# Strassen's algorithm for the first channel product of batches 4 to 7 and of the tail chunk of a fused attention and mixer kernel

## The chip, the cores and the metric

The kernel runs on one core of one Trainium2 chip. The metric is the device time of one execution in microseconds; the median of three runs of the kernel before is 276.59 us (276.38 to 277.32). A kernel is a fixed program for each engine: PE (TensorE) multiplies matrices, DVE (VectorE), ACT (ScalarE) and POOL (GpSimd) work elementwise, SP (SyncE) issues transfers. Each engine runs its own list in order, and waits on semaphores for the others.

## The reference, cut to what matters

Random-feature attention over 8 batches of 8 heads, 576 rows of 64, and then a mixer that multiplies over the rows (token product) and over the 512 channels (channel products, 512 to 1536 and back).

```python
# phi(x) = exp(x @ omega.T - |x|^2/2 - max) / sqrt(128), of q and k scaled
kv = np.einsum('bhsm,bhsd->bhmd', k_p, v)
z = np.sum(k_p, axis=2)
num = np.einsum('bhsm,bhmd->bhsd', q_p, kv)
den = np.einsum('bhsm,bhm->bhs', q_p, z)[..., None] + 1e-06
...
x = np.ascontiguousarray(attn_out.transpose(0, 2, 1, 3)).reshape(B, S, H * D)
xt = x.transpose(0, 2, 1)
h = np.maximum(xt @ w_tok1, 0.0) @ w_tok2
u = x + h.transpose(0, 2, 1)
h2 = np.maximum(u @ w_ch1, 0.0) @ w_ch2
return (u + h2).astype(np.float32)
```

## The kernel before

**Stages.** Each batch passes through attention (`attention`), the token product (`token_mix`, lines 763 to 800) and the channel products (`channel_mix`, line 955). The first 512 rows of each batch form a chunk of 512; the last 64 rows of all eight batches together form a ninth one, the tail chunk, with c equal to 8 in the code. All large operands are float16; TensorE sums in float32 in PSUM, which is handed out as eight banks of 128 x 512.

**The first channel product** (line 966) takes twelve output blocks of 128 channels. Each is four matmuls of 512 columns into one bank (weights `wc1`, moving data `t_uT`, the transposed rows), after which ACT or DVE applies the relu and writes float16 into `t_r3`.

**The second channel product** of batches 1 to 7 and of the tail (`channel_out_fast`, line 857) already goes by Strassen's algorithm: seven products of half-size matrices in place of eight, with sums of weights prepared once (`t_T`, line 448) and sums of `t_r3` made for each chunk into the single buffer `t_S` and into `t_r3` itself (line 878, through the helper on line 295). Each product is twelve matmuls of 256 columns (line 916). Three banks X, Y and Z collect the products, DVE reads them out (line 905) into `t_o`, and a transfer stores them.

**Order.** Nothing is scheduled by the framework. Every piece of work is a `Job`, added with an engine, a cost, the jobs that it depends on, and the ring places that it takes and gives back. The list `ORDER` gives the order of all jobs by their numbers (a negative one is a warming matmul), `SLOT` the places taken, and `MOVED` the jobs that run on another engine than the usual one. These three tables are the result of a planner that ran beforehand; the text of the kernel holds only its answer. Each engine gets its instructions in the sequence of `ORDER`, so a long instruction or a wait on one engine holds up everything later on it.

**Rings.** `COUNT` gives the number of buffers: 3 for the transposed q and k of a batch (`qT`, `kT`), 4 for the exponentials `qp` and `kp`, 3 for the token relu `r1`, 3 for `uT`, 2 for `r3`. The reciprocals of the attention sit in buffers that are chosen by parity (`t_km[hp % 2]`, `t_rc[2 + hp % 2]`).

**Transfers.** Chunk c's rows `t_u` (line 793, four DVE additions) are transposed by a transfer on SP's queue into `t_uT` (line 798). The same queue brings in `kT` and `qT` of later batches. POOL issues the loads of v and the casts of q and k, and between them multiplies v by its weights (`vs`, `vbd`, line 295).

Of the kernel before, what the change touches and what calls it, by code (L numbers as in the profile page):

```python
# [81 lines left out]
]  # L82
SLOT = (
    "0100234050607011034025217063304156020014123024233037016112506321174115613214067030406102530471612141"
    "6710324016307250311067345122353640751421105324100325261073641220501046112501420700521173142350120702"
    "6123534100753141200127003221065413207102503410160022357312126034171542176210025011041121126022037516"
# [82 lines left out]
def kernel(  # L169
# [27 lines left out]
    R = SM // 2  # L197
    RT = ST // 2
    RA = R + RT
    NPE = 2  # L200
    RW = S * 4 // P
    c_scale = float(1.0 / math.sqrt(math.sqrt(D)))

# [93 lines left out]
    def bank(name):  # L297
        return banks[place("bank", name)]
# [772 lines left out]
```

## Time and profile before

| | |
|---|---|
| median of 3 runs | 276.59 us |
| the profiled execution, first to last instruction | 275.9 us |
| PE busy | 266.6 us, 2503 matmuls |
| DVE busy | 222.9 us, 462 instructions |
| ACT busy | 138.1 us, 289 instructions |
| POOL busy | 91.2 us, 115 instructions |
| moved by DMA | 39.66 MB |

The profiled execution's own device time isn't given apart from its span; the runs' median lies 0.7 us above the span. Busy time is the union of an engine's instructions. On DVE the end of one instruction overlaps the start of the next by some 0.08 us, so that in a dense row the step from one start to the next is shorter than the duration. The same holds far more for PE: the duration of a matmul includes its passage through the array, and its rate is read from the length of a long row of equal ones.

### The profile page before, as it was taken

Reading aid. Unit: us, or ns where it says so; the run is one execution under the profiler, and the core shown is the slowest. Engines: PE = TensorE matmul, PEld = TensorE weight load, DVE = VectorE, ACT = ScalarE, POOL = GpSimd, SP = SyncE. Lnnn points to the kernel's source line nnn. Section 1 sums busy time; section 2 is a strip of 40 time slices with the busy share of each in tenths; the row PEclk is TensorE's granted clock in tenths of the full one; section 3 lists DMA queues with packets and bytes.
Section 4 is the critical chain, followed back from the end, with each engine's and each line's share of the span. In section 5 each row is a group of like instructions: output and inputs, shape, how many; then the busy total and the mean of one; then the engine's idle time right before and its main releaser. Section 6 shows DMA issues by size and latency. Waiting matters only on the chain.

```text
span 275.9 us, 6228 instructions
## 1 busy us (share of the span) xinstructions
PE 266.6 (97%) x2503; PEld 165.5 (60%) x2503; DVE 222.9 (81%) x462; ACT 138.1 (50%) x289; POOL 91.2 (33%) x115
## 2 busy tenths in 40 slices
PE   8789999999999999999999999999999999999993
PEld 3367455444567655755676656755676477446782
DVE  3897889876998799987999899978985992675992
ACT  3999941188685338734756456636654500040200
POOL 8994492063703490075019510600043000000001
PEclk9999999999999999999999999999999999999998
DMA  7999999999998999979989994840252304021125
GB/s 195 192 209 212 190 212 177 202 193 146 203 191 133 229 176 186 151 148 171 198 184 183 232 125 123 191 90 2 97 79 77 96 0 95 2 99 53 78 83 146
DMA packets 81292, 39.66 MB, mean 144 GB/s; under 512 B 63984, under 2 KB 77040, under 8 KB 81072
## 3 DMA queue, kind: packets, MB, share of 16 engines
q0 software_dynamic: 31744, 17.74, 44.2%
q1 hardware_dynamic: 47072, 15.50, 28.7%
q10 hardware_dynamic: 2448, 6.03, 5.6%
q8 instruction: 19, 0.31, 0.5%
q14 instruction: 9, 0.07, 0.1%
HBM read 35.95 MB, written 16.52 MB: 190 GB/s over the span
## 4 chain that ended last, share of the span: by engine, by line
PE 89%; DMA 6%; POOL 3%; DVE 0%; issue 0%; POOLq 0%
PE bank L966 33%; PE bank L916 25%; PE bank L777 5%; PE bank L790 5%; DMA w1m<-in_moe_w_tok_dram 4%; PE bank L1000 4%; PE bank L734 3%; PE bank L656 3%; PE bank L668 2%; PE bank L701 2%; DMA uT<-u 2%; POOL r L319 1%; PE bank L844 1%; PE bank L816 1%; PE bank L828 1%; PE bank L736 1%
## 5 line engine op out<-in xcount | busy, mean ns | idle before, releaser
L966 PE MATMUL bank<-uT,wc 128*128 128x512 f16 x376 | 90.4, 379 | 0.3 <-DMA uT<-u 0.3
L290 ACT ACTIVATE r<-bank 128x512 f16<-128x512 f32 (+1 forms) x84 | 46.9, 597 | 77.1 <-PE bank L966 62.0
L295 POOL TENSOR_TENSOR vs<-v,vs 128x512 f16<-128x512 f16 x31 | 33.2, 1074 | 91.2 <-DVE vs L682 60.5
L966 PEld LDWEIGHTS <-wc 128*128 128x128 f16 x424 | 38.3, 98 | 37.9 <-issue 1.1
L916 PEld LDWEIGHTS <-r 128*128 128x128 f16 x384 | 36.9, 98 | 8.1 <-issue 1.2
L514 ACT ACTIVATE kp<-bank 128x512 f16<-128x512 f32 x64 | 35.6, 622 | 10.4 <-PE bank L656 10.4
L514 ACT ACTIVATE qp<-bank 128x512 f16<-128x512 f32 x64 | 36.3, 616 | 8.9 <-PE bank L668 6.0
L680 DVE TENSOR_REDUCE km<-kp 128x8 f16<-128x1024 f16 x32 | 38.6, 1206 | 2.5 <-ACT kp L514 2.4
L292 DVE TENSOR_SCALAR r<-bank 128x512 f16<-128x512 f32 (+1 forms) x42 | 27.7, 672 | 12.0 <-PE bank L966 11.2
L744 DVE TENSOR_TENSOR x<-bank,rc 128x320 f16<-128x320 f32 x62 | 30.5, 492 | 2.1
L916 PEld LDWEIGHTS <-S 128*128 128x128 f16 x288 | 27.9, 98 | 5.4 <-issue 0.3
L905 DVE TENSOR_TENSOR o<-u,bank 128x512 f32<-128x512 f16 x28 | 19.0, 679 | 6.9 <-PE bank L916 6.8
L916 PE MATMUL bank<-T,r 128*128 128x256 f16 x192 | 23.8, 273 | 0.0
L916 PE MATMUL bank<-T,S 128*128 128x256 f16 x192 | 23.6, 273 | 0.0
L916 PE MATMUL bank<-wc,r 128*128 128x256 f16 x192 | 23.6, 273 | 0.0
L945 POOL DMA_DIRECT2D out_dram<-o x2 | 1.3, 648 | 60.9 <-issue 60.9
L793 DVE TENSOR_TENSOR u<-x,bank 128x512 f16<-128x512 f16 x28 | 17.8, 681 | 1.1 <-PE bank L790 1.0
L905 DVE TENSOR_TENSOR o<-o,bank 128x512 f32<-128x512 f32 (+1 forms) x27 | 16.6, 618 | 2.2 <-PE bank L916 1.6
L734 PEld LDWEIGHTS <-qp 128*128 128x128 f16 x256 | 13.8, 98 | 7.0 <-DVE kvsb L286 0.2
L734 PE MATMUL bank<-kvsb,qp 128*128 128x65 f16 x256 | 15.6, 193 | 0.0
L743 DVE RECIPROCAL rc<-bank 128x5 f32<-128x5 f32 x62 | 11.5, 186 | 4.1 <-PE bank L736 2.7
L701 PEld LDWEIGHTS <-kp 128*128 128x128 f16 x256 | 11.5, 98 | 5.1
(120 smaller groups left out, 376.3 us busy)
## 6 DMA issues: line engine op xcount, KB each, us to landing
out_dram<-o ACTq DMA_DIRECT2D x9, 512.0 KB, 2.6
q<-in_q_dram POOLq DMA_DIRECT2D x6, 576.0 KB, 7.2
wc<-in_moe_w_ch_dram POOLq DMA_DIRECT2D x4, 768.0 KB, 10.6
k<-in_k_dram POOLq DMA_DIRECT2D x6, 512.0 KB, 6.9
v<-in_v_dram POOLq DMA_DIRECT2D x6, 512.0 KB, 8.9
out_dram<-o SPq DMA_DIRECT2D x5, 512.0 KB, 3.9
r<-in_q_dram POOLq DMA_DIRECT2D x4, 288.0 KB, 7.3
v<-in_v_dram POOLq DMA_DIRECT2D x4, 256.0 KB, 8.7
```

The source lines that it names most:

```text
L290: nc.scalar.activation(out=out, in_=in_, func=AF.Relu)
L292: nc.vector.tensor_relu(out=out, in_=in_)
L295: (nc.gpsimd if eng == "POOL" else nc.vector).tensor_tensor(**kw)
L514: nc.scalar.activation(out=out, in_=in_, func=AF.Exp, bias=0.0, scale=1.0)
L680: nc.vector.reduce_max(out=mx, in_=kpv, axis=AX.X)
L701: nc.tensor.matmul(ps[:, i, :], kpv[:, 2 * i + j // 2, j % 2, :], vs[:, i * NJ + j, 0 : D + 1], start=(i == 0 and j == 0), stop=False, ski ...
L734: nc.tensor.matmul(ps[:, k, j * 65 : (j + 1) * 65], st, s[:, i, 0 : D + 1], start=True, stop=True)
L744: nc.vector.tensor_tensor(out=t_x[place("x", b)][:, :, (2 * hp + hs[0]) * D : (2 * hp + hs[0] + n) * D].rearrange("p j (i d) -> p i j d", ...
L793: nc.vector.tensor_tensor(out=t_u[place("u", b)][:, j, :], in0=t_x[place("x", b)][:, j, :], in1=bank(n), op=ALU.add)
L905: nc.vector.tensor_tensor(out=o, in0=a, in1=ps, op=ALU.add)
L916: nc.tensor.matmul(ps[:, j * DH : (j + 1) * DH], a[:, cb, j * P : (j + 1) * P], w[:, cb, :], start=(bank_of(b, j0) not in held and j == j0 ...
L966: nc.tensor.matmul(ps, wc1[:, db, cb * P : (cb + 1) * P], moving(db), start=(db == 0), stop=(db == ND - 1))
```

## The change

**The first channel product of chunks 4 to 8** no longer runs as 48 matmuls of 512 columns. A new function `channel_in_fast` splits rows, inner and outer dimension in halves and forms seven products P1 to P7 in place of eight, in three groups of 256 output channels. Each product of a group is four matmuls of 256 columns. Bank X takes P1, then P6 on top of it, P7 on top of both, and P4 at last; ACT copies what stands in X after each of the first three to SBUF in float32, because the next product changes it. Y takes P2, Z takes P5 and P3. DVE adds each copy to the bank that belongs to it (`join`) and the relu follows: of one quarter straight from the bank, of the other three on float16 in SBUF. The copies of P1 go into the part of `r3` that the same group fills later, the others into places of the `qp` and `kp` rings.

**Sums.** Four sums of blocks of `uT` are made for each chunk, in a place of the `uT` ring, and four sums of weights (in two parts each) once for all, in `weight_sums`: three parts in a place of `qT`, three in one of `kT`, held until the end, and two in a new buffer.

**The rest.** `r1` has 2 places in place of 3. Reciprocals `km`, `kmt` and `rc` become ring buffers with 4, 2 and 8 places, taken and given back by jobs, and the reciprocal and the scaling become jobs of their own; the scaling may go to ACT. The tail's output uses places of `x` in place of `o`. The sums of the second product have looser dependences among them. `ORDER`, `SLOT` and `MOVED` are new throughout; with them 13 of the 64 sums of the second product move from DVE to POOL, 5 of the 8 sums of weights and 11 of the 20 sums of `uT` are put there, and 35 more scalings of 128 x 64 run on ACT. The branches for `SPLIT` and `HALVES` aren't taken, since both are empty.

```diff
+    FAST_IN = 4
+    SPLIT = ()
+    HALVES = ()
...
-             "kvsb": 3, "ktt": 2, "x": 3, "r1": 3, "u": 3, "uT": 3, "r3": 2, "S": 1, "o": 2, "bank": 8}
+             "kvsb": 3, "ktt": 2, "x": 3, "r1": 2, "u": 3, "uT": 3, "r3": 2, "S": 1, "o": 2, "km": 4, "rc": 8, "kmt": 2, "bank": 8}
...
+    def weight_sums(key):
...
+        steps = (((1, 0), (1, 1), ALU.add), (0, (0, 0), ALU.subtract), ((0, 0), (1, 0), ALU.subtract), ((0, 1), 1, ALU.subtract))
+        for a in range(2):
+            done = []
+            for i, (x, y, op) in enumerate(steps):
+                e_sum = engine("DVE")
...
+    def channel_in_fast(c, key, jt):
...
+        ops = {
+            "P1": ("X", weights(0, 0), lambda: block(0, 0), []),
+            "P2": ("Y", weights(0, 1), lambda: block(1, 0), []),
+            "P5": ("Z", sum_weights(0), lambda: sums()[:, 0], [j_sums[0][0], j_sums[1][0], j_s[0]]),
+            "P6": ("X", sum_weights(1), lambda: sums()[:, 1], [j_sums[0][1], j_sums[1][1], j_s[1]]),
+            "P7": ("X", sum_weights(2), lambda: sums()[:, 2], [j_sums[0][2], j_sums[1][2], j_s[2]]),
+            "P4": ("X", weights(1, 1), lambda: sums()[:, 3], [j_s[3]]),
+            "P3": ("Z", sum_weights(3), lambda: block(1, 1), [j_sums[0][3], j_sums[1][3]]),
+        }
...
+                            nc.tensor.matmul(ps[:, n, :], w(a)[:, (2 * m + n) * P : (2 * m + n + 1) * P], x_[:, a],
+                                             start=(what in ("P1", "P2", "P5") and n == 0 and a == 0), stop=False, skip_group_check=True)
...
+            p1 = product("P1", [])
+            p2 = product("P2", [])
+            p5 = product("P5", [])
+            k1 = keep("P1", "X", p1)
+            c11 = join("P1", "Y", 0, 0, [k1, p2], True)
+            p6 = product("P6", [k1])
+            k2 = keep("U2", "X", p6)
+            p7 = product("P7", [k2])
+            k3 = keep("U3", "X", p7)
+            c22 = join("U3", "Z", 1, 1, [k3, p5, c11], False)
+            p3 = product("P3", [c22])
+            c12 = join("U2", "Z", 0, 1, [k2, p3], True)
+            p4 = product("P4", [k3])
...
     def channel_mix(c, key, jt):
...
+        if c >= FAST_IN:
+            channel_out_fast(c, key, channel_in_fast(c, key, jt))
+            return
...
+        if b == FAST_IN:
+            weight_sums(b - 1.0)
```

More of the change, by code (lines that the diff above doesn't have):

```diff
@@ L598, in kt_max @@
                 )
-            j_ktm = add("DVE", 1.2, kkt + 0.01, kt_max, deps=[*j_kte, j_msk], take=[("vbd", b)] if dma_in else [])
+            j_ktm = add("DVE", 0.15, kkt + 0.01, kt_mask, deps=[j_ktm, j_msk], take=take_vbd, give=[("kmt", b)])
             def vbd():
@@ new lines, in rec, with scale @@
+                def rec(hp=hp, i=hs[0], where=where):
+                    nc.vector.reciprocal(out=t_rc[place("rc", (b, hp, i))], in_=where()[:, 0, 0 : 5 * 65].rearrange("p (j d) -> p j d", d=65)[:, :, D])
+                j_r = add("DVE", 0.1, kno, rec, deps=[j_n], take=[("rc", (b, hp, hs[0]))])
+                e_num = engine("DVE")
+                def scale(hp=hp, i=hs[0], where=where, e_num=e_num):
+                    to = t_x[place("x", b)][:, :, (2 * hp + i) * D : (2 * hp + i + 1) * D]
+                    ps = where()[:, 0, 0 : 5 * 65].rearrange("p (j d) -> p j d", d=65)[:, :, 0:D]
+                    rc = t_rc[place("rc", (b, hp, i))]
+                    if e_num == "ACT":
+                        for j in range(NJ + 1):
+                            nc.scalar.activation(out=to[:, j], in_=ps[:, j], func=AF.Copy, scale=rc[:, j : j + 1])
+                    else:
+                        nc.vector.tensor_tensor(out=to, in0=ps, in1=rc.unsqueeze(2).broadcast_to((P, NJ + 1, D)), op=ALU.mult)
@@ L762, in attention @@
+                last_x.append(add(e_num, 0.45, kno, scale, deps=[j_r], take=[("x", b)], give=[at, ("rc", (b, hp, hs[0]))]))
         return last_x
@@ L865, in channel_out_fast @@
             part = slice(g * NH // 2, (g + 1) * NH // 2)
-            need = [jr[cb + NH * e] for cb in range(part.start, part.stop) for e in range(2)]
+            need = [x for cb in range(part.start, part.stop) for e in range(2) for x in jr[cb + NH * e]]
             steps = (
@@ L878, in go @@
                     tt(e_sum, out=o[:, part], in0=a[:, part], in1=b[:, part], op=op)
[L879 to L880 removed]
+                job = add(e_sum, 0.5, key + KEYS["S"] + 0.1 * g + 0.01 * k, go, deps=[*need, *([done[2 if k == 3 else 0]] if k else [])], take=[("S", c)])
+                done.append(job)
                 sums.setdefault(i, []).append(job)
@@ L897, in bank_of, with o_tag, o_of, go @@
             return (b, c, j0) if tail else (b, c)
+        def o_tag(i):
+            return ("x", ("o", i)) if tail else ("o", (c, i))
+        def o_of(i):
+            if tail:
+                return t_x[place(*o_tag(i))].rearrange("p j d -> p (j d)")[:, 0 : 4 * DM].bitcast(FP32).rearrange("p (j d) -> p j d", j=2)
+            return t_o[place(*o_tag(i))]
         def read(k, b, i, e, base, deps, free, j0=0, j1=2):
-            def go(c=c):
-                o = t_o[place("o", (c, i))][:, j0:j1, DH * e : DH * e + DH]
+            e_read = engine("DVE")
+            def go(c=c, e_read=e_read):
+                o = o_of(i)[:, j0:j1, DH * e : DH * e + DH]
                 ps = bank(bank_of(b, j0)).rearrange("p (j d) -> p j d", j=2)[:, j0:j1]
+                if e_read == "ACT":
+                    nc.scalar.copy(out=o, in_=ps)
+                    return
                 u = t_u[place("u", c)] if c < B else t_ut
@@ L905, in go, with late_base, base_in @@
                 nc.vector.tensor_tensor(out=o, in0=a, in1=ps, op=ALU.add)
-            return add("DVE", 0.345 * (j1 - j0), key + KEYS["c2"] + step * k, go, deps=deps, take=[("o", (c, i))],
+            return add(e_read, 0.345 * (j1 - j0), key + KEYS["c2"] + step * k, go, deps=deps, take=[o_tag(i)],
                        give=([("bank", bank_of(b, j0))] if free else []) + ([("u", c)] if base and c < B else []))
+        def late_base(k, i, e, x, deps):
+            e_base = engine("POOL")
+            def base_in(c=c, x=x, e_base=e_base):
+                if outs[x, 0].eng == "DVE":
+                    return
+                o = o_of(i)[:, :, DH * e : DH * e + DH]
+                tt(e_base, out=o, in0=t_u[place("u", c)][:, 2 * i : 2 * i + 2, DH * e : DH * e + DH], in1=o, op=ALU.add)
+            return add(e_base, 1.1, key + KEYS["c2"] + step * k, base_in, deps=deps, give=[("u", c)])
         outs, j_z = {}, {}
@@ L944, in store @@
                         to = out[4 * i : 4 * i + 4, SM:S, cols].rearrange("(j h) t d -> h t j d", h=2)[h]
-                        (nc.scalar if eng == "ACT" else nc.sync if eng == "SP" else nc.gpsimd).dma_start(out=to[:, js], in_=t_o[place("o", (c, i))][half[h], js, cols])
-                    dma(eng, key + 0.9, 0.3, store, deps=[outs[need, j] for j in range(*js)], give=[("o", (c, i))],
+                        (nc.scalar if eng == "ACT" else nc.sync if eng == "SP" else nc.gpsimd).dma_start(out=to[:, js], in_=o_of(i)[half[h], js, cols])
+                    dma(eng, key + 0.9, 0.3, store, deps=[outs[need, j] for j in range(*js)], give=[o_tag(i)],
                         cost=0.412 if js[1] - js[0] == 1 else 0.414)
@@ L951, in store @@
             def store(i=i, eng=eng):
-                (nc.scalar if eng == "ACT" else nc.sync).dma_start(out=out[c, 0:SM, :].rearrange("(p j) d -> p j d", j=NJ)[:, 2 * i : 2 * i + 2, :], in_=t_o[place("o", (c, i))])
-            dma(eng, key + 0.9 + 0.1 * i, 1.3, store, deps=[outs[x, 0] for x in need], give=[("o", (c, i))], cost=0.4)
+                (nc.scalar if eng == "ACT" else nc.sync).dma_start(out=out[c, 0:SM, :].rearrange("(p j) d -> p j d", j=NJ)[:, 2 * i : 2 * i + 2, :], in_=o_of(i))
@@ L984, in relu @@
                 relu_to(e_relu, t_r3[place("r3", c)][:, cb, :], bank(n))
-            jr[cb] = (add(e_relu, 0.5, key + 0.5 * pos / NCB, relu, deps=[j1], take=[("r3", c)], give=[("bank", n)]))
+            jr[cb] = [add(e_relu, 0.5, key + 0.5 * pos / NCB, relu, deps=[j1], take=[("r3", c)], give=[("bank", n)])]
         if fast:
@@ L1001, in channel_mix @@
                 prev = add("PE", mm(4, 512) + (mm(4, P) if part == 2 else 0.0), key + 0.5 + 0.5 * (3 * j + part) / 12, c2,
-                           deps=[prev, *jr[4 * part : 4 * part + 4], *j_wc2], take=[("bank", n)], give=[("r3", c), ("uT", c)])
+                           deps=[prev, *(x for done in jr[4 * part : 4 * part + 4] for x in done), *j_wc2], take=[("bank", n)], give=[("r3", c), ("uT", c)])
             k2 = key + 0.5 + 0.5 * (3 * j + 3) / 12
```

208 lines of the change are left out of this document (150 added, 58 removed), and 131 rows, old and new, of the table ORDER.

## The prediction

> **What bounds the kernel now.** I read the page first, then the chain of work that ended last in order of time.
>
> ```profile
> span 275.9 us, 6228 instructions
> PE 266.6 (97%) x2503; PEld 165.5 (60%) x2503; DVE 222.9 (81%) x462; ACT 138.1 (50%) x289; POOL 91.2 (33%) x115
> PE 89%; DMA 6%; POOL 3%; DVE 0%; issue 0%; POOLq 0%
> ```
> ```profile
> 83.37 5.98 DMA uT<-u
> ...
> 234.09 13.81 PE bank L966 x64
> ...
> 260.94 10.51 PE bank L916 x96
> 271.48 0.42 DVE o L905
> ```
>
> The chain is TensorE almost throughout. Two of its long rows give the rates: a matmul of 512 columns takes 13.81 / 64 = 0.2158 us, one of 256 columns 10.51 / 96 = 0.1095 us. The other engines appear with the head's loads, with one transposing transfer (5.98 us from the last addition of `u` to the first matmul on it) and with the last read. The stretches from the end of one batch's token product to the next's show how near the others come:
>
> ```profile
> 109.86:139.12 29.26, 29.26 (x294) 18.73 (x293) 25.80 (x54) 17.44 (x38) 9.58 (x11) 1.00 0.95 172
> 139.12:167.34 28.22, 28.22 (x266) 17.93 (x265) 25.77 (x56) 15.06 (x31) 12.19 (x14) 1.00 1.05 181
> 167.34:196.46 29.12, 29.12 (x274) 18.26 (x273) 25.45 (x52) 16.26 (x34) 4.86 (x5) 1.00 0.44 101
> 196.46:224.50 28.04, 28.04 (x260) 17.73 (x259) 23.44 (x50) 13.16 (x27) 5.20 (x5) 1.00 0.30 67
> 224.50:275.90 51.40, 46.94 (x336) 32.64 (x334) 32.66 (x61) 5.92 (x11) 1.29 (x2) 0.98 0.25 75
> ```
>
> The columns are the stretch, then busy PE, weight loads, DVE, ACT and POOL, and the clock. PE is never idle in four of them, at full clock; DVE is busy for 100.5 of 114.6 us there (88%), ACT for 54% and POOL for 28%. So a saving on TensorE counts in full until DVE becomes the later one. That is the question of this change.
>
> **TensorE.** Five chunks lose 48 matmuls of 512 columns each and gain 84 of 256 (seven products, three groups, four matmuls): 240 x 0.2158 = 51.8 us go and 420 x 0.1095 = 46.0 us come, together **-5.8 us**. The new ones load weights as often as those of L916, whose loads hide:
>
> ```profile
> L916 PEld LDWEIGHTS <-r 128*128 128x128 f16 x384 | 36.9, 98 | 8.1 <-issue 1.2
> ```
>
> 98 ns stand under 109.5 ns of matmul. If that cover went, the 11 ns of difference show how little it would need, but the same pair already runs at the rate above. PE's other work keeps its sizes, and its order is much the same up to the token product of batch 2.
>
> **DVE.** Durations overlap, so I take steps from one start to the next:
>
> ```profile
> 216.02 0.49 DVE L744 TENSOR_TENSOR x<-bank,rc 128x320 f16<-128x320 f32 x1
> 216.42 0.18 DVE L743 RECIPROCAL rc<-bank 128x5 f32<-128x5 f32 x1
> 223.43 1.88 DVE L793 TENSOR_TENSOR u<-x,bank 128x512 f16<-128x512 f16 x3
> ```
> ```profile
> 248.18 0.55 DVE L295 TENSOR_TENSOR S<-S,r 128x768 f16<-128x768 f16 x1
> 248.65 0.55 DVE L295 TENSOR_TENSOR r<-r 128x768 f16<-128x768 f16 x1
> ```
> ```profile
> L292 DVE TENSOR_SCALAR r<-bank 128x512 f16<-128x512 f32 x40 | 26.9, 684 | 11.7 <-PE bank L966 11.2
> L905 DVE TENSOR_TENSOR o<-o,bank 128x512 f32<-128x512 f32 x21 | 14.1, 674 | 1.6 <-PE bank L916 1.1 <-issue 0.2
> L680 DVE TENSOR_REDUCE km<-kp 128x8 f16<-128x1024 f16 x32 | 38.6, 1206 | 2.5 <-ACT kp L514 2.4
> L545 DVE COPY ktt<-kT 128x256 f16<-128x256 f16 x1 | 0.2, 227 | 0.0
> ```
>
> Three additions with a PSUM operand of 512 take 1.88 us and one lasts 0.68, so the step is (1.88 - 0.68) / 2 = 0.60 us; the scaling steps by 0.40, a sum of 768 float16 values in SBUF by 0.47, which is 0.61 ns per value. Away go 20 relus from PSUM (12.0 us), 13 sums of the second product (6.1) and 7 scalings (2.8): 20.9 us. There come 45 joins, float32 with a bank as the L905 row (27.0), one relu from PSUM (0.6), three sums of weights (1.4), nine sums of 512 of `uT` (2.8), and seven relus each of 1024 and 512 values in SBUF. The trace has no such relu. Below, the copy of 256 values in 0.23 us bounds each; above, the reduction of 1024 with 1.21 us and the 0.68 us row for 512. At 0.61 ns per value they are 0.63 and 0.31, together 6.6 us (bounds 3.2 and 13.2). In all DVE gains 38.4 - 20.9 = **17.5 us** (14 to 24). Counted by the order of the two programs, some 4 of it fall between the token products of batches 3 and 7, where TensorE's share shrinks by 6 at the same time, and the rest behind. There DVE goes from 88% busy to 96%, and in the last stretch from 32.7 to about 46 of some 51 us. It still fits, barely, and only if nothing is late.
>
> **ACT and POOL.**
>
> ```profile
> 205.90 3.09 POOL L295 TENSOR_TENSOR vs<-v,vs 128x512 f16<-128x512 f16 x3 [0.42 <-DVE vs L682]
> ```
> ```profile
> 208.08 1.58 ACT L290 ACTIVATE r<-bank 128x512 f16<-128x512 f32 x3
> ```
> ```profile
> L756 ACT ACTIVATE x<-bank,rc 128x64 f16<-128x64 f32 x10 | 2.3, 340 | 0.0
> ```
>
> ACT steps by 0.49 us for 512 values, POOL by 1.02 (three in 1.58 and in 3.09, less one of 0.60 and of 1.06). ACT gains 45 copies and loses 26 relus from banks, 9.3 us; 35 short scalings add 8.0 at 0.23 each, and eight relus each of 1024 and 512 values in SBUF some 10 at its own rate: 27 us onto 68 of the last 166, no bound. POOL gains 18 sums of 768 (1.52 each) and 11 of 512, 38.6 us onto 33.1 of 166: not a bound either, but its sums feed products of TensorE, and it issues the loads of v and the casts behind them in the same list. The cover is POOL's idle time, 82.8 of the 114.6 us of the four stretches; if it failed, whatever stands behind a sum would come 1.52 us later for each.
>
> **Where TensorE now waits.** I followed three places in the new order.
>
> (1) The sums S2 of chunk 6. Between the last P3 of that chunk and the first matmul on the second half of S2, TensorE has 8 matmuls on half rows, 8 of 512 and 47 of 256 columns: 0.4 + 1.7 + 5.1 = 7.2 us. In that time DVE has two joins, six additions from PSUM, two sums S1, a read of the output and three sums: 9 x 0.60 + 5 x 0.47 = 7.8 us. It is 0.6 us late.
>
> (2) The transfer of chunk 7. It begins with the last addition of `u`, which ends 1.5 us behind the last token product since DVE has the joins ahead of it. At 5.98 us it lands 7.5 us behind; TensorE has 60 matmuls of 256 columns, 6.6 us, and the 0.6 of (1). That leaves 0.3 us.
>
> (3) The tail's S2. POOL makes S1 and S2 of one half, 2 x 1.52 = 3.0 us, behind a relu on ACT that comes after three long ones. TensorE reaches the first matmul on it about 0.7 us earlier.
>
> That is 1.6 us. Chunks 4, 5 and the start of 6 have the same pattern with attention between to fill it; I add 0.9, so **+2.5 us**. Bounds are 0 (all hidden, as before the change) and 0.6 in each of 15 groups, 9.0.
>
> **Edits at nothing.** The reciprocals' ring takes a wait off DVE at most: 0 to -0.5 us, covered by TensorE. The second place less of `qT`, `kT` and `r1` makes transposed loads on SP wait for TensorE's use two batches back; the uT transfer stands behind them on the same queue. The cover is that these loads are due a batch ahead; without it the 5.98 us of the transfer would be late once more, and TensorE with it.
>
> **Sum.** Span 275.9 - 5.8 + 2.5 = 272.6 us. The runs' median is 276.59, 0.7 above the profiled span, so 273.3 us is expected for the median.
>
> **Rivals.** *No new waits.* The order hides everything as the old one did: 275.9 - 5.8 + 0.7 = 270.8 us. For it speaks that TensorE is never idle in four stretches with DVE at 88%, against it the three places above. Chance 0.18.
>
> *The chain within a group eats the saving.* Each group goes product, copy, product, copy, product, copy, join, product, join, relu: 4 x 0.44 us of products, 3 x 0.60 of copies and 3 x 0.68, with a change of engine at nine steps, so over 5.6 us, while it holds up to three of eight banks. If other work does not fill it, 15 groups each lose 0.4 us: 6.0 in place of 2.5 gives 276.8 us, no change. Chance 0.13.
>
> *DVE and POOL stop each other (slower).* In the one place of the head where both multiply data in SBUF at once, POOL's product took 0.44 us longer:
>
> ```profile
> 14.52 1.02 DVE L295 TENSOR_TENSOR vs<-v,vs 128x512 f16<-128x512 f16 x1
> ...
> 14.96 1.50 POOL L295 TENSOR_TENSOR vs<-v,vs 128x512 f16<-128x512 f16 x1
> ```
>
> Elsewhere the old kernel hardly puts the two at once: its POOL products run in the attention, its sums behind. The new one gives POOL 29 sums, and DVE has 26 sums and relus of float16 in SBUF between the token products of batches 3 and 7. If each of those waits for half a POOL sum, 0.75 us, DVE gets 19.5 us more; some 11 of them is the room that is left, and 8.5 go to TensorE: 275.9 - 5.8 + 8.5 + 0.7 = 279.3 us. It decides from about nine hits on above the room, 6.6 us of new waits. Against it speaks that many of these sums wait for one another anyway. Chance 0.15.
>
> The Trainium skill (SBUF — State Buffer, Who interferes with whom) states this as a rule: a VectorE instruction with two inputs in SBUF and a GpSimd instruction that reads SBUF exclude each other, and the second to issue waits for the whole of the first. The trace agrees as far as its one case goes: 0.44 us longer with 0.58 us of the DVE product left.
>
> **How the numbers follow.** The forecast has 0.50 (271.8 to 275 us, its waits between 1 and 4), the rivals 0.18, 0.13 and 0.15, and 0.04 is left for others. What a measurement tells from no change is 0.3%, 275.8 to 277.4 us. Faster: 0.50 + 0.18 + 0.02 = 0.70; same 0.13; slower 0.15 + 0.02 = 0.17. The range 270.5 to 277.8 takes in the forecast, both nearer cases and a weak form of the last.
>
> **What would show it.** In the new profile the 84 matmuls per chunk should step by 0.110 us, and PE's sum fall by 5.8. DVE should be over 90% busy from batch 3's token product on, and the joins take 0.67 us each. The chain should show DVE or POOL ahead of the second products of chunks 6 and 8, for under 1 us each, and the transfer of chunk 7. POOL sums of 768 far above 1.5 us, or DVE sums above 0.56, would speak for the third rival; many gaps ahead of P6, P7 and P3 for the second. A TensorE that waits at the start of a chunk for a transposed load would prove the last edit wrong.

## The result and the profile after

The changed kernel takes 279.03 us (median of 20 runs, 277.1 to 283.04), the kernel before 277.25 (20 runs, 276.38 to 278.96). The ratio is 1.0047, with a 95% interval of 1.0024 to 1.007; it leaves out runs far above a kernel's fastest, so it lies below the quotient of the medians. The change is slower, where 273.3 us and faster was forecast. The profiled execution took 278.83 us at a span of 277.1.

The page of the changed kernel, its busy times and its chain by engine and by line:

```profile
span 277.1 us, 6721 instructions
PE 262.4 (95%) x2683; PEld 183.8 (66%) x2683; DVE 236.0 (85%) x493; ACT 168.3 (61%) x360; POOL 132.5 (48%) x144
PE 72%; DMA 11%; DVE 11%; ACT 2%; POOL 1%; issue 1%; POOLq 0%; DVEq 0%; SPq 0%
```

The five stretches from the end of one batch's token product to the next's, and from the last to the end, in the columns of the prediction:

```profile
109.35:142.23 32.88, 31.95 (x337) 20.14 (x336) 30.32 (x63) 24.78 (x60) 28.39 (x27) 1.00 1.06 164
142.23:168.81 26.58, 23.67 (x250) 18.77 (x248) 21.69 (x44) 16.49 (x41) 12.77 (x13) 1.00 0.97 171
168.81:197.10 28.29, 26.87 (x288) 20.49 (x289) 25.75 (x55) 19.82 (x44) 15.97 (x14) 1.00 0.61 89
197.10:224.52 27.42, 27.27 (x299) 21.37 (x297) 25.04 (x54) 18.55 (x35) 10.93 (x10) 1.00 0.31 68
224.52:277.06 52.54, 47.32 (x432) 42.01 (x430) 43.72 (x87) 17.55 (x30) 6.36 (x5) 0.98 0.28 84
```

TensorE, which filled four stretches before, has holes now: 0.93, 2.91 and 1.42 us in the first three. By its busy share DVE is not the cover that ran out: it is busy for 102.8 of the 115.2 us of the four stretches, 89% as against 88%. What TensorE waited for between 105 and 270 us, with the total, the number of times and the longest wait (the same view of the kernel before has no row there):

```profile
PE bank L572 <- DMA kT<-k: 2.9, 1, 2.9
PE bank L962 <- DVE S L316: 1.2, 1, 1.2
PE bank L817 <- DVE r L313: 0.7, 1, 0.7
PE bank L692 <- DVE u L820: 0.2, 1, 0.2
PE bank L1145 <- DMA uT<-u: 0.2, 1, 0.2
```

That is 5.2 us. The chain in order of time has their places, and a row with the rate of the new products:

```profile
133.75 12.95 DMA kT<-k
...
172.15 2.36 DVE S L316 x2
174.56 1.48 PE bank L962 x12
...
243.73 5.68 PE bank L1074 x52
...
265.14 6.72 PE bank L962 x60
271.89 0.42 DVE x L942
```

The transposed keys of batch 6 land 12.95 us after their issue, where the kernel before has 6.1. The view of that transfer in the kernel before:

```profile
L380 SPq DMA_TRANSPOSE kT<-k x1: 3683/3683/3683, 136.7 to 136.7; - x1
...
DMA to landing us min/median/max: 6.1/6.1/6.1
```

At 172 us two sums on DVE take 2.36 us in place of 1.0. From the end of batch 3's token product to the last matmul there are 162.5 us (109.35 to 265.14 + 6.72) where there were 161.6: 5.8 less of matmuls by their rates, and so, by subtraction, 6.7 more of waits, of which the view of the waits shows 5.2. (It leaves out the short ones, and a wait is shorter in it than the step from matmul to matmul: 2.9 us for a gap of 3.07.) The rest of the 1.2 us in span is 0.5 less ahead of that stretch and 0.8 more behind the last matmul.

Where POOL issued the loads of k and v of batch 7, in the timeline of the kernel before and then of the changed one, whose last row is SP's issue of `kT` of batch 6:

```profile
146.92 0.55 POOL L364 DMA_DIRECT2D k<-in_k_dram  x1
147.46 0.91 POOL L337 DMA_DIRECT2D v<-in_v_dram  x1
```
```profile
137.03 0.58 POOL L385 DMA_DIRECT2D k<-in_k_dram  x1
137.60 0.91 POOL L358 DMA_DIRECT2D v<-in_v_dram  x1
...
133.75 6.41 SPq L401 DMA_TRANSPOSE kT<-k  x1
```

The old order has the loads behind the transposing transfers `kT` of batch 6 and `uT` of batch 4, the new one among them.

### The profile page after: what moved, and what is told of

Read it like the earlier page. It is cut to its first block, busy times and chain, and to the rows that moved or that the text cites. A ratio compares the mean times of both kernels' runs of the same rounds, so it can differ in the third digit from the quotient of the medians.

```text
span 277.1 us, 6721 instructions
## 1 busy us (share of the span) xinstructions
PE 262.4 (95%) x2683; PEld 183.8 (66%) x2683; DVE 236.0 (85%) x493; ACT 168.3 (61%) x360; POOL 132.5 (48%) x144
## 4 chain that ended last, share of the span: by engine, by line
PE 72%; DMA 11%; DVE 11%; ACT 2%; POOL 1%; issue 1%; POOLq 0%; DVEq 0%; SPq 0%
PE bank L962 21%; PE bank L1074 15%; PE bank L1145 12%; DMA kT<-k 5%; DMA uT<-u 4%; PE bank L1179 4%; PE bank L804 3%; PE bank L769 2%; PE bank L817 2%; DVE u L820 2%; DMA r<-in_q_dram 2%; PE bank L736 2%; PE bank L680 2%; DVE S L316 2%; PE bank L692 1%; DVE r L1098 1%
## 5 line engine op out<-in xcount | busy, mean ns | idle before, releaser
L311 ACT ACTIVATE r<-bank 128x512 f16<-128x512 f32 (+1 forms) x58 | 33.3, 595 | 24.2 <-PE bank L1145 13.0
L1145 PE MATMUL bank<-uT,wc 128*128 128x512 f16 x184 | 44.9, 379 | 0.2 <-DMA uT<-u 0.2
L787 DVE TENSOR_TENSOR x<-bank,rc 128x320 f16<-128x320 f32 x55 | 26.4, 486 | 1.2
L1145 PEld LDWEIGHTS <-wc 128*128 128x128 f16 x184 | 16.3, 98 | 16.1 <-issue 1.1
L1074 PE MATMUL bank<-uT,wc 128*128 128x256 f16 x156 | 22.1, 273 | 0.1
L316 POOL TENSOR_TENSOR S<-r 128x768 f16<-128x768 f16 x4 | 6.5, 1640 | 28.5 <-PE bank L962 28.5
L316 POOL TENSOR_TENSOR S<-r,S 128x768 f16<-128x768 f16 x8 | 13.2, 1660 | 13.9 <-DVE S L316 13.9
L1074 PEld LDWEIGHTS <-wc 128*128 128x128 f16 x180 | 17.0, 98 | 2.9 <-issue 0.4
L316 POOL TENSOR_TENSOR vbd<-vt,vbd 128x512 f16<-128x512 f16 x6 | 6.4, 1058 | 26.0 <-DVE vbd L617 25.7
L313 DVE TENSOR_SCALAR r<-bank 128x512 f16<-128x512 f32 (+1 forms) x23 | 15.1, 662 | 3.9 <-PE bank L1145 3.1
L942 DVE TENSOR_TENSOR o<-o,bank 128x512 f32<-128x512 f32 x21 | 14.1, 674 | 4.6 <-PE bank L962 4.3
```

The lines of the kernel that those rows point to most:

```text
L311: nc.scalar.activation(out=out, in_=in_, func=AF.Relu)
L313: nc.vector.tensor_relu(out=out, in_=in_)
L316: (nc.gpsimd if eng == "POOL" else nc.vector).tensor_tensor(**kw)
L787: nc.vector.tensor_tensor(out=to, in0=ps, in1=rc.unsqueeze(2).broadcast_to((P, NJ + 1, D)), op=ALU.mult)
L942: nc.vector.tensor_tensor(out=o, in0=a, in1=ps, op=ALU.add)
L1074: nc.tensor.matmul(ps[:, n, :], w(a)[:, (2 * m + n) * P : (2 * m + n + 1) * P], x_[:, a], start=(what in ("P1", "P2", "P5") and n == 0 and ...
```

## The experiments

Three theories: Q (in the first four texts D), the transposing transfers on SP's queue land late because they share the DMA engines with the loads and casts that POOL issues and with the stores; L, a sum on POOL and a sum on DVE stop each other, and POOL's sums are long; C, DVE has too much work. R is the rival to Q that the place less in the rings of `qT` and `kT` makes it. A gap is the step from the start of one matmul to the next less the usual step, so that before `kT` it is 3.07 us where the view says 2.9. In the table of the runs the ratio is to the kernel before, and the waits are the sum of the view shown above (for a4, whose end comes later, up to 285 us), in one profiled execution each. The profiled executions of a1 (291.23 us, its median 284.96) and of d3 (282.47, its median 279.67) stand for themselves and not for what the ratio measures. Landing is from issue, of `kT` of batch 6 and `uT` of batch 4.

| run | ratio | waits, us | kT, uT landing, us |
|---|---|---|---|
| before | 1 | 0 | 6.1, 4.7 |
| after | 1.0047 [1.0024, 1.007] | 5.2 | 12.95, 7.9 |
| a1 | 1.0257 [1.0221, 1.0294] | 9.6 | 11.7, 13.7 |
| a2 | 0.9998 [0.9972, 1.0024] | 3.0 | 9.0, 6.6 |
| a3 | 1.026 [1.0224, 1.0296] | 8.2 | 16.5, 12.2 |
| a4 | 1.0294 [1.0252, 1.0336] | 9.7 | 9.0, 13.7 |
| a5 | 1.0012 [0.9987, 1.0038] | 4.2 | 11.9, 4.8 |
| a6 | 0.9999 [0.9971, 1.0028] | 3.0 | 9.9, 6.1 |
| a7 | 1.0017 [0.9991, 1.0044] | 4.8 | 11.3, 6.2 |
| b1 | 1.0127 [1.0096, 1.0158] | 2.6 | 11.1, 6.4 |
| c1 (work left out) | 0.993 [0.9897, 0.9963] | 1.9 | 9.7, 6.2 |
| c2 (work left out) | 0.9993 [0.9977, 1.0009] | 3.3 | 9.0, 6.1 |
| c3 (work left out) | 0.992 [0.99, 0.9939] | 1.7 | 9.0, 6.2 |
| c4 | 1.0087 [1.0057, 1.0116] | 4.1 | 13.5, 6.2 |
| d1 | 0.9994 [0.9971, 1.0018] | 2.7 | 9.1, 6.2 |
| d2 | 1.0195 [1.0159, 1.0231] | 8.6 | 16.6, 13.0 |
| d3 | 1.004 [1.0012, 1.0068] | 7.4 | 10.4, 4.6 |
| f1 | 0.9994 [0.9978, 1.001] | 2.9 | 5.8, 6.1 |
| f2 | 0.999 [0.9968, 1.0012] | 3.3 | 5.0, 6.1 |
| f3 | **0.9946 [0.992, 0.9972]** | 1.7 | 5.1, 6.2 |

### a1 to a4: the loads, the stores, the sums

In `ORDER`, 1189 and 1194 are the loads of k and v of batch 7, 748 and 1015 the transfers of `uT` of batch 4 and `kT` of batch 6, 498 and 497 the stores of chunk 2.

```diff
 a1
-    736, 633, 1189, 873, 877, 1194, 631, 739,
+    736, 633, 873, 877, 631, 739,
...
-    895, 867, 748, 1046, 1080,
+    895, 867, 748, 1189, 1194, 1046, 1080,
 a2
-    697, 860, 498, 733, 620,
+    697, 860, 1015, 498, 733, 620,
...
-    872, 893, 1015, 878, 910,
+    872, 893, 878, 910,
 a3 (MOVED)
-    752: "POOL", 809: "POOL", 813: "POOL", 1421: "POOL", 1423: "POOL",
```

a4 makes all three edits.

> The loads of k and v of batch 7 are issued by POOL behind the transfer of uT of batch 4, in place of 6 us ahead of it, as the kernel before had them; nothing else is moved. Theory D (queue): kT of batch 6 lands 12.95 us after its issue because these loads, a q cast and two stores share the DMA engines with it. It then lands within 7 us, the 3.07 us gap at its first matmul (146.74 us) goes to under 0.5 us and the time falls by 2 to 3 us against the changed kernel: ratio to the kernel before 0.994 to 0.998. Theory L (DVE and POOL stop each other): DVE is the later one there, the gap is only handed to DVE's sums behind it, and the ratio stays at 1.003 to 1.006. Theory C (all of DVE too late): the same as L.

> SP issues kT of batch 6 ahead of the two stores of chunk 2, in place of behind them; POOL's loads stay. Theory D in the form 'what stands ahead on SP': the load is issued at some 129 us in place of 133.75 and lands before 142, even if the landing takes 10 us, so the 3.07 us gap goes and the ratio is 0.994 to 0.998. Theory D in the form 'a full place': its place of the ring is still read by TensorE and it is issued at 133 us again, nothing changes (1.003 to 1.006). Theories L and C: the gap goes but the time doesn't follow, 1.003 to 1.006.

> Five of POOL's sums that overlap a sum of DVE's go back to DVE at their old place of the order (one sum of weights, two S sums of chunk 4, two of the tail). Theory L: the DVE sums that took 1.63, 1.96 and 1.65 us take 0.55 again; DVE makes five sums more at 0.47 us but loses 3.6 us of waits, so the stalls of 0.89 (140.15 us), 1.38 (174.56) and 0.18 us (265.14) shrink by 1.5 to 2.4 us in all: ratio 0.996 to 1.001. Theory C: DVE is too late by its work as such; with 2.4 us more of it the stalls grow, 1.005 to 1.010. Theory D: no change of the 3.07 us gap, and little of the time (1.002 to 1.005).

> The three edits together. Theories D and L add up: the changed kernel less 3 and less 2 us, ratio 0.985 to 0.990, some 273.5 us where the kernel before has 277.2; that is the forecast of the prediction. Theory C: no gain over the best of the three alone.

a2 agreed with Q in direction: `kT` lands at 138.8 us, ahead of its use, and 1.3 us of the time come back (1.0047 to 0.9998; the two intervals just touch). Of the 3.07 us gap 1.06 us is handed on to `uT` of batch 4. a1 missed: with the loads moved on by 13 us the collision is now with `uT`, which takes 13.7 us, and `kT` still takes 11.7 us without them. a4, which holds a1's edit, missed in the same way: `uT` takes 13.7 us there too, and TensorE waits 8.0 us for it. a1's timeline of TensorE, and its windows with the granted clock behind POOL's busy time:

```profile
163.41 2.74 PE L1179 MATMUL bank<-uT,wc 128*128 128x256 f16 x12 [6.08 <-DMA uT<-u]
165.95 2.41 PE L1067 MATMUL bank<-T,r 128*128 128x256 f16 x12
```
```profile
155.00:160.00 5.00, 2.34 (x33) 1.90 (x30) 4.33 (x12) 0.25 (x1) 0.00 (x0) 1.00 1.32 126
160.00:165.00 5.00, 1.59 (x8) 1.15 (x9) 0.00 (x0) 0.00 (x0) 1.49 (x2) 0.60 1.51 125
165.00:170.00 5.00, 5.00 (x42) 3.95 (x41) 1.57 (x5) 2.79 (x9) 4.97 (x6) 0.72 0.97 137
```

The wait costs 6.1 us and then the clock: twelve matmuls take 2.74 us, where elsewhere they take 1.31. a3 missed by a late `kT`, not as Theory C has it: without its sum POOL issues the load of k at 136.31 us in place of 137.03, and `kT`, issued at 133.3, lands after 16.5 us. Where they were in its reach the sums did what L says, since the waits for DVE's sums fell from 0.89 to 0.33 us at 140 and from 1.38 to 0.87 at 175 us; on the tail they rose from 0.18 to 0.78.

In the changed kernel, in a3 and in d2 (below) `kT` lands within 0.2 us of that load of k: at 146.70 and 146.52, 149.78 and 149.60, 150.86 and 150.81 us.

### a5 to a7 and b1: the loads out of the way, and into it

1018 is the load of v of batch 6. a6 is a5 with a2's move of 1015; a7 is a6 with 752, 809 and 813 taken out of `MOVED`. b1 moves the same two loads in the kernel before (1003 and 1008 in its numbers), which has nothing of the change.

```diff
 a5
-    736, 633, 1189, 873, 877, 1194, 631, 739,
+    736, 633, 873, 877, 631, 739,
...
-    920, 801, 1018, 802, 1028,
+    920, 801, 1018, 1189, 1194, 802, 1028,
 b1
-    583, 870, 768, 589, 779,
+    583, 870, 1003, 1008, 768, 589, 779,
```

> POOL issues the loads of k and v of batch 7 only behind the load of v of batch 6 (about 157 us), when uT of batch 4 and qT of batch 6 have landed; kT stays behind the stores. Theory Q (the transposing transfers share the DMA engines with POOL's loads; a1 only moved the loads from kT onto uT and qT): kT of batch 6 lands in 6 to 9 us, uT of batch 4 in under 6.5, qT in under 7; the gaps at 146.7 and 150 us are under 1 us together, the clock stays at 0.995 or above: ratio to the kernel before 0.990 to 0.997. Rival R (a transposing transfer of the new order is slow of itself, by the ring's lost place): kT lands in over 10 us again and the ratio is over 1.003.

> a5 with kT of batch 6 ahead of the two stores on SP as in a2. Theory Q: kT is 4 us early and in nobody's way, uT of batch 4 (6.57 us in a2) lands in under 6, so the 1.06 us gap of a2 at 150 us goes: ratio 0.988 to 0.995, and less spread from run to run than the changed kernel's 275.3 to 281.2. Rival R: as a2, 0.999 to 1.002.

> a6 with the sum of weights and the two S sums of chunk 4 on DVE, which a3 gave 0.56 and 0.51 us less of stall; the tail's sums stay on POOL since a3 lost 0.60 us by them. Theory L (a POOL sum and a DVE sum stop each other): 0.8 to 1.2 us less than a6, ratio 0.985 to 0.991. Theory C (DVE too late by its work): the same as a6 or slower.

> The kernel before (no Strassen in the first product) with its loads of k and v of batch 7 issued at 128 us in place of 147, ahead of POOL's products of batch 5. Theory Q: kT of batch 6 (6.07 us) or uT of batch 4 (4.71 us) then lands in over 9 us, TensorE, which had no gap there, waits 2 to 6 us, and the ratio is 1.007 to 1.03: the loss comes with the order of the transfers, whatever the algorithm. Rival R: the landings and the time stay (0.998 to 1.003).

b1 is the plainest answer. Its timeline of POOL and its waits of TensorE in the same window:

```profile
127.50 0.57 POOL L444 DMA_DIRECT2D k<-in_k_dram  x1
128.05 0.93 POOL L417 DMA_DIRECT2D v<-in_v_dram  x1
```
```profile
PE bank L631 <- DMA kT<-k: 2.6, 1, 2.6
```

The old kernel with its three full places per ring loses 1.27% by the place of two loads: Q holds, and the loss needs no place less in a ring. Not all of the 3.5 us is the wait: behind it the clock is at two thirds for 5 us (see the last section). R falls with f1 to f3 below, where `kT` lands in 5.0 to 5.8 us though the place is still missing. In a5 `uT` is quick again (4.8 us) but `kT`, beside the stores and the q cast, still takes 11.9, so its own bound of 6 to 9 us was wrong. So the two loads account for little of the 12.95 us in the changed kernel: without them `kT` takes 11.7 (a1) and 11.9 us (a5), ahead of the stores 9.0 to 9.9 (a2, a6), and with the q cast behind it as well 5.0 to 5.8 (f1 to f3). In a6 both land nearly in time, with no better median than a2: the gaps at 140 and 172 us are left. a7 didn't gain, as Theory C had forecast: a wait of 1.8 us for DVE's additions to `u` took the place of the first, and two for `uT` of batches 4 and 5 (2.1 us together; the second transfer took 7.1 us) came beside what was left of the second, 0.7 us. c2 below tests C apart.

### c1 to c4: what the sums and the joins cost

c1 and c3 narrow the sums on POOL, c2 and c3 thirty joins; the rest of those sums and joins is left out. c1, c3 and c4 move the sum of weights 752, which stood beside DVE's sums, behind 632. c4 keeps all work: a6 with 752 moved, 809 and 813 on DVE and both stores of chunk 2 on ACT.

```diff
 c1
-                    tt(e_sum, out=o[:, part], in0=a[:, part], in1=b[:, part], op=op)
+                    n = 32 if e_sum == "POOL" else 2 * P
+                    tt(e_sum, out=o[:, part, 0:n], in0=a[:, part, 0:n], in1=b[:, part, 0:n], op=op)
...
-    625, 621, 752, 697, 860,
+    625, 621, 697, 860,
...
-    896, 1081, 632, 912, 626,
+    896, 1081, 632, 752, 912, 626,
 c2
+                    w = 32 if i == 0 else 256
-                    nc.vector.tensor_tensor(out=r3(i, j, m), in0=kept(what, m).rearrange("p (n t) -> p n t", n=2), in1=pair(b, m), op=ALU.add)
+                    nc.vector.tensor_tensor(out=r3(i, j, m)[:, :, 0:w], in0=kept(what, m).rearrange("p (n t) -> p n t", n=2)[:, :, 0:w], in1=pair(b, m)[:, :, 0:w], op=ALU.add)
```

> a6 with POOL's S sums and sums of uT cut to 32 and 16 columns of each row piece (an eighth of the work; the rest is left out), and the sum of weights that met DVE's (135.69 us in a6) moved behind the last S sum of chunk 3. No POOL sum is then long enough to hold DVE. Theory L (DVE and POOL stop each other): the DVE sums of 1.99 and 2.42/2 us go back to 0.55, the gaps of 1.33 us (140.2) and 1.36 us (172.3) shrink to under 0.4 each: ratio 0.991 to 0.995. Theory C (DVE too late by its own work): the gaps stay above 1 us, ratio 0.997 to 1.001. Theory Q (transfers): the same as C, with the gaps at 150 and 202 us.

> a6 with 30 of the 45 joins cut to 32 of 256 columns in each half (c11 and c12; the rest of them is left out): about 14 us less of DVE's work, of the 17.5 that the change added. Theory C: TensorE's waits fall to the level of the kernel before, ratio 0.985 to 0.991. Theory L: only the DVE sums' hits count, which stay: 0.996 to 1.000. Theory Q: uT starts some 0.5 us earlier for each transfer that has joins ahead of it, 0.994 to 0.998.

> Both cuts together: what is left is the transfers' share and the order's. If Theories L and C hold all of the 4.8 us of waits that a6 has over the kernel before, 0.980 to 0.984; if half of it is the transfers, 0.988 to 0.992.

> A whole kernel again: a6 with the two stores of chunk 2 on ACT's queue (in a6 they stand behind kT and DVE waits 0.48 us for one), the sum of weights behind the S sums as in c1, and two S sums of chunk 4 on DVE. Theories L and Q: 1 to 2 us less than a6, ratio 0.992 to 0.997. Theory C: as a6, 0.998 to 1.002.

TensorE's waits in c1 and then in c2:

```profile
PE bank L1181 <- DMA uT<-u: 1.1, 2, 0.7
PE bank L841 <- DVE u L925: 0.8, 1, 0.8
```
```profile
PE bank L1067 <- DVE S L421: 1.5, 1, 1.5
PE bank L922 <- DVE r L418: 0.7, 1, 0.7
PE bank L1179 <- DMA uT<-u: 0.6, 2, 0.4
PE bank L1251 <- DMA uT<-u: 0.5, 1, 0.5
```

POOL's sums, with the move of 752, are worth 0.7% (0.9999 to 0.993, 1.9 us): without them no wait for a sum `S` is left. c2 takes 11.8 us off DVE's busy time (235.4 in a6 to 223.6, the level of the kernel before) and gains nothing, and c3 is not clearly better than c1. Theory C falls, at least for the joins. c4 is a miss: on ACT's queue the stores start beside `kT` (at 131.4 us), which then takes 13.5 us.

### d1 to d3: shorter sums on POOL

d1 is a6 with 752 moved, d2 the changed kernel and d3 a2 with it; in all three POOL makes each S sum in three instructions.

```diff
-                    tt(e_sum, out=o[:, part], in0=a[:, part], in1=b[:, part], op=op)
+                    step = 1 if e_sum == "POOL" else NH // 2
+                    for s in range(part.start, part.stop, step):
+                        tt(e_sum, out=o[:, s : s + step], in0=a[:, s : s + step], in1=b[:, s : s + step], op=op)
```

> A whole kernel: a6, with the sum of weights moved as in c1, and each S sum on POOL made as three instructions of 256 values in place of one of 768. Theory L, by whole instructions: a DVE sum then waits for at most a third of a POOL sum (0.55 us), so of c1's gain of some 1.9 us two thirds come: the gaps at 140 and 172 us are 0.3 to 0.7, ratio 0.993 to 0.997. If DVE has to wait until POOL's queue of sums is empty, the ratio stays at 0.998 to 1.002, as a6.

> The changed kernel with its transfers as they are, and only the sum of weights moved and POOL's S sums in three. Theory L alone: the gap at 174.6 us (1.38) and that at 140.2 (0.89) shrink to under 0.7 and 0.4, the 3.07 us gap before kT of batch 6 stays: ratio 1.000 to 1.003 where the changed kernel has 1.0047. If the late kT hides what DVE gains in front of it, only the later one counts: 1.002 to 1.004.

> As d1, but with POOL's loads of batch 7 where the changed kernel has them (a2 with the sums in three). Theories L and Q add up: a2's 0.9998 less 0.4 to 0.7%, 0.993 to 0.996. If the loads of batch 7 still collide with uT of batch 4 (1.06 us of gap in a2), it is 0.2% above d1.

A DVE sum beside POOL's in the timelines, DVE's row and POOL's in a6, then DVE's at 170 us in d1 and d3's addition at 146 us:

```profile
136.06 1.99 DVE L421 TENSOR_TENSOR S<-r 128x768 f16<-128x768 f16 x1
...
135.69 1.95 POOL L421 TENSOR_TENSOR sum<-wc,qT 128x768 f16<-128x768 f16 x1
```
```profile
170.32 1.01 DVE L421 TENSOR_TENSOR S<-S,r 128x768 f16<-128x768 f16 x1 [0.15 <-POOL S L421]
172.51 0.56 DVE L421 TENSOR_TENSOR S<-S,r 128x768 f16<-128x768 f16 x1 [1.18 <-POOL S L421]
```
```profile
146.24 0.69 DVE L1049 TENSOR_TENSOR o<-u,bank 128x512 f32<-128x512 f16 x1 [6.52 <-DMA out_dram<-o]
```

These rows fit a lock by whole instructions: 1.99 us beside a sum of 768, 1.01 beside sums of 256, 0.55 alone. One row of f2 doesn't: there a DVE sum of 768 at 137.46 us takes 2.09 us beside three sums of 256, so how long DVE is held isn't settled. And the time did not follow (0.9994 to a6's 0.9999): in d1 DVE's next sum has POOL's sum as its input and waits 1.18 us for it. So at this place the plain length of POOL's sums counts beside the lock, and c1 had cut both. d2 missed by 2%: its load of k went out at 136.82 us against 137.03, and `kT` took 16.6 us. d3 missed too (1.004 for 0.993 to 0.996). Its profiled execution shows a further way to lose: a store of chunk 2, behind `kT` on SP and beside the loads, takes 8.7 us, DVE waits 6.52 us for the place in `o`, and TensorE for DVE. That one execution doesn't explain the ratio.

### f1 to f3: an order by reasons

1011 and 1017 are the cast of q and rows of v of batch 6, 1187 the cast of q of batch 7, 936 and 937 sums of `uT` of batch 5. The sums are in three, and 752 and 1015 as in d1. f1 also has 809 and 813 on DVE, f2 leaves them on POOL.

```diff
 f1, f2: moved
-    850, 730, 1011, 494, 695, 904, 1017, 849,
+    850, 730, 494, 695, 904, 849,
...
-    619, 859, 876, 890, 696,
+    619, 859, 876, 1011, 1017, 890, 696,
...
-    920, 801, 1018, 802, 1028,
+    920, 801, 1018, 1189, 802, 1028,
...
-    1062, 939, 936, 1191, 1057,
+    1062, 939, 936, 1187, 1194, 1191, 1057,
 f3: beside f2
-    936, 1187, 1194, 1191,
+    936, 1187, 1191,
...
-    1071, 940, 812, 944,
+    1071, 940, 937, 1194, 812, 944,
...
-    908, 854, 754, 622,
+    908, 854, 622,
...
-    748, 1046,
+    748, 754, 1046,
```

> A whole kernel with the transfers kept apart by reason: kT of batch 6 ahead of the stores and of the q cast of batch 6 (which goes behind POOL's two products of batch 5), k of batch 7 behind v of batch 6, q and v of batch 7 only behind uT of batch 5; POOL's S sums in three, the sum of weights late, and the two S sums of chunk 4 that others wait for on DVE. Theories Q and L together: kT lands in under 8 us, uT of batches 4 and 5 in under 6.3, the gaps from 139 to 177 us sum to under 2.5 us (a6: 3.8): ratio 0.990 to 0.996. If moving a load only moves the collision, as in a1, 0.998 to 1.003.

> f1 with the two S sums of chunk 4 on POOL as the changed kernel has them. If the gap at 172 us (1.93 in d1) is the plain length of POOL's sums, which DVE's next sum takes as input, it stays at 1.3 to 2.0 us and the kernel is 0.5 to 1.2 us behind f1. If it was the lock alone, the sums in three have cured it and the two are equal.

> A whole kernel: f2, with the sum of weights on DVE that took 2.09 us beside a POOL sum (137.46 us) moved behind the transfer of uT of batch 4, and the third sum of uT of batch 5, for which TensorE waited 1.17 us at 185.5, ahead of the last S sums on POOL and of the load of v of batch 7. Theory L: the gap at 142.7 us (1.82) shrinks to under 0.6 and that at 185.5 (1.34) to under 0.4, about 2 us in all; f2 less 1.5 to 2.2 us gives a ratio of 0.991 to 0.995, faster than both kernels. If every place given up only opens the next gap, 0.997 to 1.001.

The waits of TensorE in f2, then in f3:

```profile
PE bank L922 <- DVE r L418: 1.9, 2, 1.7
PE bank L1181 <- POOL uT L421: 1.2, 1, 1.2
PE bank L1069 <- DVE r L421: 0.2, 1, 0.2
```
```profile
PE bank L922 <- DVE r L418: 0.6, 2, 0.3
PE bank L1069 <- DVE r L421: 0.6, 1, 0.6
PE bank L1252 <- DMA uT<-u: 0.5, 1, 0.5
```

f1 and f2 keep the landings at 5 to 6.2 us, the first ones to do so, but not the time, for gaps opened behind two sums that now stood badly. f2 came out as was expected for the lock alone, since the gap at 172 us is gone and the two kernels are equal; but it doesn't decide. DVE comes to its sum there at 172.24 us, when POOL's six short sums have all but ended (172.34); in d1 it came at 170.32, and POOL was at them until 172.48. f3 moves those two sums, and the load of v of batch 7 behind the second of them, and is faster than the kernel before and the changed one, 275.71 us against 277.27 of the kernel before, with all the work in it. Its gain over f2 (0.9946 against 0.999) is at the edge of the two intervals.

## Why the prediction was wrong, point by point

**TensorE, right.** 52 of the new matmuls take 5.68 us, 0.109 each, so that the 5.8 us are gone from its list. The weight loads hide. The sign given for it, PE's sum less by 5.8, didn't come: the busy time fell by 4.2 us (266.6 to 262.4), as a part of each wait hides in it behind the duration of the matmul ahead (the gap of 3.07 us counts as 2.9).

**The sizes on ACT and POOL, nearly right; DVE's too high.** From the groups of the changed kernel:

```profile
L1098 DVE TENSOR_TENSOR r<-qp,bank 128x512 f16<-128x512 f32 x15 | 10.1, 682 | 1.7 <-PE bank L1074 1.6
...
L313 DVE TENSOR_SCALAR r<-r 128x1024 f16<-128x1024 f16 (+1 forms) x14 | 5.5, 408 | 0.1
...
L316 POOL TENSOR_TENSOR S<-r,S 128x768 f16<-128x768 f16 x8 | 13.2, 1660 | 13.9 <-DVE S L316 13.9
```

A join lasts 0.68 us as forecast, the 14 relus sum to 5.5 us for 6.6, and a POOL sum of 768 lasts 1.66 for 1.52. POOL's busy time grew by 41.3 us for 38.6, ACT's by 30.2 for 27 (eight relus each of 1024 and 512 values at 0.49 us per 512 are 11.8 us, where the sum has "some 10"). DVE's grew by 13.1 us (236.0 less 222.9) for 17.5, below the stated 14 to 24, though some 4.4 of it are the hits named below; which of its terms was too high wasn't taken apart. It is busy for 89% of the four stretches, not over 90%.

**"That is the question of this change": wrong.** Taking 11.8 us of joins off DVE (c2) changed nothing. How much of DVE is busy was the wrong question; which of its instructions stands in front of a wait was the right one.

**"Edits at nothing": the step that failed.** The prediction saw that transposed loads might be late and named as their cover that they "are due a batch ahead". It asked about the ring places alone, and gave the new order of the transfers, a part of the change ("new throughout"), no price. `kT` of batch 6 was issued 13 us ahead of its first matmul, which is cover for the 6 us that it takes alone and not for the 12.95 that it takes beside two stores, a cast and two loads. The wait is 2.9 us in the profile, and a2, a5 and a6 bring 1.0 to 1.4 us of the 4.6 us between forecast and result (-3.3 and +1.3), though their intervals touch or overlap that of the changed kernel; b1 makes a loss of 3.5 us out of the same thing in the old kernel, a part of it by the clock. The mechanism that the sentence had, loads that wait for a place in their ring, was not the one at work: with the place still missing `kT` lands in time in f1 to f3.

**"No bound" for POOL, and the third rival: the mechanism right, the count wrong.** POOL's sums cost 1.9 us (c1). In place of 26 hits of 0.75 us there were four of 0.8 to 1.4 (three DVE sums of 1.63, 1.96 and 1.65 us, one relu of 1.23); the first two stand ahead of TensorE's waits at 140 and 175 us. That this rival's 279.3 us lies next to the measured 279.03 is luck: a late transfer, which it didn't have, makes up for the hits that didn't come. By the rule that the prediction took from the Trainium skill (SBUF — State Buffer, Who interferes with whom) the second to issue waits for the whole of the first. a6's 1.99 us against d1's 1.01 agrees with it; f2's 2.09 us beside short sums doesn't follow from it. The prediction left out what d1 shows: a POOL sum, three times as long as DVE's, also keeps the DVE sum that has it as an input.

**The new waits, "+2.5 us": too small, and wrong in place.** Without the late `kT` (a gap of 3.07 us) some 3.6 of the 6.7 us of waits are left in the changed kernel. In a6, where `kT` is in time, the way from the end of batch 3's token product to the last matmul is 160.35 us (109.4 to 269.75), so 4.6 us of waits by the same subtraction; the view shows 3.0 of them. So of the 4.2 us of waits above the forecast 2.1 went with a6's moves, and 2.1 stayed: this term was mis-sized by as much as the late transfer cost, and a6 comes back to the kernel before and not to the forecast. None of the waits shown is at chunks 6 and 7 as traced by hand, the tail's is 0.18 us for 0.7; the rest is in chunks 4 and 5 and ahead of them, where the prediction had only its "I add 0.9".

**The chain within a group** doesn't show: the view of the changed kernel has no row for the line of the new products, L1074.

**The base of the sum.** The 0.7 us from span to time compared one execution with the median of others. In each run where both are listed the time is 1.7 to 2.0 us above its own span, so the forecast's 272.6 us of span would have been some 274.4 us of time.

**What is open.** f3 has 1.5 us of the 3.3 us that were forecast. Waits of 1.7 us are left in its view, more in gaps too short for it, and some 0.6 us behind the last matmul; no run took these apart. The runs of the changed kernel spread from 275.3 to 281.2 us in span, the times of the kernel before mostly within 1 us; that a few tenths of a us in POOL's order move `kT` by 3.6 us (d2 against the changed kernel) is a likely reason, but the spread itself was not traced.

## What to carry to other kernels

Where a change re-plans an order, price the order: list each transfer that the bounding engine waits for with what else is in flight from its issue to its use, before and after, and take its cover against the landing in company, not alone. A spare engine's work is not free when its results feed, or its instructions lock out, the engine that stands in front of the bound. Undo single moves of the order first: it is a cheap experiment, and here one move (a2) gave back 1.3 us, where cutting POOL's sums in three (d1) gave nothing. But look at the landings each time, since a move can also shift the collision to the next transfer, as in a1, which lost 2.1% more.

## What the runs showed of the hardware that was not expected

A transposing transfer that gets in front of a load by 2.6 to 3.3 us doesn't end in front of it: it lands within 0.2 us of that load, in three kernels, after 12.95 to 16.6 us in place of 6. The Trainium skill (DMA: Bandwidth & Descriptors, Queues, rings and completion order) says that each DMA engine takes turns between its queues by packets, which would fit these landings. No run here looks at packets, and without that load beside it `kT` still took 11.7 and 11.9 us (a1, a5).

A wait on TensorE can have a second price. b1's wait of 2.6 us was followed by two windows of 2.5 us with a granted clock of 0.65 and 0.67, which by these figures is some 1.7 us more; around the waits of 6.1 to 8.0 us in a1, a3, a4 and d2 the clock went down to 0.50 for at least one such window. After the changed kernel's wait of 2.9 us it stays at 1.00. The windows of b1, then of the changed kernel:

```profile
147.50:150.00 2.50, 2.50 (x20) 1.87 (x19) 0.82 (x3) 1.64 (x4) 1.92 (x3) 0.65 1.27 202
150.00:152.50 2.50, 2.50 (x21) 1.89 (x19) 0.67 (x2) 0.00 (x0) 2.50 (x4) 0.67 1.66 282
```
```profile
145.00:150.00 5.00, 3.26 (x50) 2.93 (x51) 1.07 (x3) 2.43 (x6) 0.56 (x1) 1.00 1.37 190
150.00:155.00 5.00, 5.00 (x59) 4.53 (x58) 5.00 (x13) 1.96 (x8) 3.40 (x4) 1.00 1.08 162
```

So the length of the single wait does not decide it, as it fell behind the shorter one and not behind the longer one; what does, no run here took apart.
